# A first MLP product of 20 block products instead of 24, and a list schedule for the whole program

## The chip, the cores and the metric

The kernel runs on one core of one Trainium2 chip. The metric is device time in microseconds (us): the median over several executions. The span of a profile is a little shorter than the time of its run (608.1 for 609.9), because the time also covers start and end.

## The reference, cut to what matters

A gated linear attention (a recurrence over 768 steps, for 4 x 8 heads of 48) makes x of 3072 tokens by 384. An MLP with a hard-swish gate follows. Everything is float32.

```python
state = alpha[:, :, t, :, None] * state + einsum('bhd,bhde->...', k[:, :, t], v[:, :, t])
y[:, :, t] = np.einsum('bhd,bhde->bhe', q[:, :, t], state)
...                                     # y becomes x, 3072 x 384
h = x @ w_in                            # 384 x 2048: the first product
g = h * np.clip(h + 3.0, 0.0, 6.0) / 6.0
return g @ w_out                        # 2048 x 384: the second product
```

(The first line is shortened.) The tokens go through the kernel in 24 blocks of 128, called tokens below, two to a group, so there are 12 groups.

## The kernel before

In groups 2 to 11 the first product is plain: for each of eight pairs of 128 hidden columns, three matmuls (384 = 3 x 128) of 256 tokens into one bank, then the gate on ScalarE and the multiply on VectorE. The second product runs already as seven block products on halves.

```python
def ff1(g, i):
    h = ps_t["h", g, i] = ps.tile([C, 2, GT], FP, tag="h", bufs=2, name="h_ps")
    for f in range(2):
        for kk in range(KT):
            o = (2 * i + f) * C
            nc.tensor.matmul(h[:, f], w1[:, kk, o : o + C], xT_t[g][:, kk],
                             start=(kk == 0), stop=(kk == KT - 1))
```

A fixed loop orders the program. The loads of token n+1 are issued ahead of the scans of token n; the attention steps of the token before stand in two places of a group, and each of the eight steps of a first product is followed by one of the second product of the group before.

```python
for g in range(2, NG + 1):
    for i in range(8):
        n = G * (g + 2) + i // 4
        if i % 4 == 0 and n + 1 < NCH:
            run("la.{0} lk.{0} lq.{0} lv.{0}".format(n + 1))
        if i % 4 == 0 and n < NCH:
            run("ca.{0} r.{0} k.{0} p.{0} q.{0}".format(n))
        ...
        if g < NG:
            run("f.{0}.{1} fr.{0}.{1} fg.{0}.{1}".format(g, i))
        if i < 7:
            product(g - 1, i)
```

So the products of two groups alternate, and while VectorE and ScalarE work on one, TensorE has the other.

## Time and profile before

| | before |
|---|---|
| time, median | 609.27 us (609.22 to 609.82, 3 runs) |
| span of the profile, mean granted clock | 608.1 us, 1.000 |
| TensorE, VectorE, ScalarE, GpSimd busy | 97%, 60%, 22%, 8% |
| distance of groups | 47.7 us |

```profile
SPq L513 <- DVE o L511: 246.9, 33, 17.9
```

The clock is full in every slice. The queue stands 246.9 us before stores that wait for VectorE's results (L513 is the store). That costs nothing here: its loads come a token early. Of VectorE's waits, all those for a transfer sum to 1.5 us.

### The profile page before, as it was taken

The page shows a single profiled execution, that of the slowest core. Times are in us where ns is not written, and L with a number is a line of the kernel's source. Part 1 is how long each engine was busy: PE and PEld are TensorE (multiplying, and loading weights), DVE is VectorE, ACT ScalarE, POOL GpSimd, SP SyncE. Part 2 cuts the span into 40 slices and gives each one's busy share as a digit, 9 for nine tenths or more (in the row PEclk, how much of TensorE's full clock was granted, in tenths as well). Part 3 has the DMA queues.
Part 4 walks back from the last instruction along what each step waited for, and adds up shares of the span by engine and source line. Part 5 has one row for each costly group of instructions (what it writes and reads, how often), then busy time and mean ns, then how long its engine had stood idle before and what let it go on. Part 6 is the DMA issues. An engine that isn't in the chain of part 4 may idle for free.

```text
span 608.1 us, 10549 instructions
## 1 busy us (share of the span) xinstructions
PE 588.9 (97%) x4416; PEld 527.5 (87%) x4416; DVE 362.1 (60%) x493; ACT 135.3 (22%) x227; POOL 49.8 (8%) x78
## 2 busy tenths in 40 slices
PE   6778999999999999999999999999999999999998
PEld 4667887679999998999999998999999999999997
DVE  7698979869877577467467477357446224115141
ACT  1555445011121111111111211112111111112110
POOL 2234323201000000000000000000000000000000
PEclk9999999999999999999999999999999999999999
DMA  9999998324354243132131131130000000000000
GB/s 161 195 221 183 182 237 167 90 74 94 94 126 103 67 99 83 36 80 60 40 98 44 30 75 44 29 77 13 9 14 8 8 15 7 9 19 8 6 14 27
DMA packets 90384, 44.74 MB, mean 74 GB/s; under 512 B 54752, under 2 KB 85216, under 8 KB 90336
## 3 DMA queue, kind: packets, MB, share of 16 engines
q1 hardware_dynamic: 90336, 44.06, 33.4%
q8 instruction: 35, 0.57, 0.4%
q14 instruction: 13, 0.11, 0.1%
HBM read 39.32 MB, written 4.72 MB: 72 GB/s over the span
## 4 chain that ended last, share of the span: by engine, by line
PE 81%; DVE 0%; ACT 0%; issue 0%
PE h_ps L408 35%; PE x_ps L503 19%; PE y_ps L503 14%; PE sc_ps L314 3%; PE y_ps L378 3%; PE o_ps L430 2%; PE u_ps L356 2%; PE y_ps L388 2%; PE kb_ps L331 1%; DVE raw L196 0%; DVE q L306 0%; PE tq_ps L255 0%; ACT o L509 0%
## 5 line engine op out<-in xcount | busy, mean ns | idle before, releaser
L408 PE MATMUL h_ps<-xT,w 128*128 128x256 f32 x1152 | 265.8, 382 | 7.7 <-POOL w L201 7.7
L408 PEld LDWEIGHTS h_ps<-xT,w 128*128 128x128 f32 x1152 | 214.0, 190 | 39.5 <-POOL w L201 9.6
L418 DVE SCALAR_TENSOR_TENSOR g_sb<-r,h_ps 128x512 f32<-128x512 f32 x96 | 65.6, 684 | 149.4 <-ACT r L413 149.0
L413 ACT ACTIVATE r<-h_ps,half 128x512 f32<-128x512 f32 x96 | 66.0, 687 | 224.2 <-PE h_ps L408 219.6
L503 PE MATMUL x_ps<-rings,g_sb 128*128 128x192 f32 x352 | 60.8, 326 | 0.0
L503 PE MATMUL y_ps<-w,g_sb 128*128 128x192 f32 x352 | 60.8, 326 | 0.0
L503 PEld LDWEIGHTS x_ps<-rings,g_sb 128*128 128x128 f32 x352 | 58.4, 190 | 1.0
L503 PEld LDWEIGHTS y_ps<-w,g_sb 128*128 128x128 f32 x352 | 58.4, 190 | 1.0
L341 POOL TENSOR_TENSOR t<-t,R 128x384 f32<-128x384 f32 x20 | 18.3, 917 | 388.6 <-DVE t L368 255.4
L320 DVE TENSOR_TENSOR A<-sc_ps,mask 128x512 f32<-128x512 f32 x48 | 30.9, 685 | 15.3 <-PE sc_ps L314 15.3
L282 DVE TENSOR_TENSOR_SCAN R<-t,ones 128x516 f32<-128x516 f32 x24 | 31.2, 1304 | 11.7 <-POOL t L341 9.1
L314 PEld LDWEIGHTS sc_ps<-q,k 48*128 48x128 f32 x384 | 24.7, 197 | 7.9 <-issue 5.9
L293 DVE TENSOR_TENSOR_SCAN P<-t 128x516 f32<-128x516 f32 x24 | 31.0, 1294 | 0.5
L314 PE MATMUL sc_ps<-q,k 48*128 48x128 f32 x384 | 29.4, 295 | 1.1 <-DVE q L306 1.1
L503 PE MATMUL x_ps<-rings,s 128*128 128x192 f32 x176 | 30.4, 326 | 0.0
L503 PE MATMUL y_ps<-w,s 128*128 128x192 f32 x176 | 30.4, 326 | 0.0
L503 PE MATMUL x_ps<-w,g_sb 128*128 128x192 f32 x176 | 30.4, 326 | 0.0
L503 PEld LDWEIGHTS x_ps<-w,g_sb 128*128 128x128 f32 x176 | 29.2, 190 | 0.6
L503 PEld LDWEIGHTS y_ps<-w,s 128*128 128x128 f32 x176 | 29.2, 190 | 0.5
L503 PEld LDWEIGHTS x_ps<-rings,s 128*128 128x128 f32 x176 | 29.2, 190 | 0.5
L396 ACT COPY xT<-y_ps 128x384 f32<-128x384 f32 x24 | 11.5, 478 | 79.3 <-PE y_ps L388 66.9
L378 PE MATMUL y_ps<-A,t 128*32 128x128 f32 x768 | 27.0, 282 | 0.3 <-DVE A L320 0.3
(76 smaller groups left out, 491.1 us busy)
## 6 DMA issues: line engine op xcount, KB each, us to landing
raw<-in_moe_w_out_dram SPq DMA_DIRECT2D x8, 768.0 KB, 4.7
t<-in_v_dram SPq DMA_DIRECT2D x48, 96.0 KB, 3.4
raw<-in_moe_w_in_dram SPq DMA_DIRECT2D x24, 192.0 KB, 7.0
out_dram<-o SPq DMA_DIRECT2D x44, 96.0 KB, 1.7
aq<-in_alpha_dram SPq DMA_DIRECT2D x32, 96.0 KB, 2.4
raw<-in_k_dram SPq DMA_DIRECT2D x32, 96.0 KB, 2.3
raw<-in_q_dram SPq DMA_DIRECT2D x32, 96.0 KB, 2.3
aq<-in_alpha_dram SPq DMA_DIRECT2D x32, 80.0 KB, 2.2
```

What stands on the lines that cost most here:

```text
L282: nc.vector.tensor_tensor_scan(out=reverse(R, n - 1, n), data0=reverse(ax, n, n), data1=reverse(ones, n, n), initial=0.0, op0=ALU.mult, op ...
L293: nc.vector.tensor_tensor_scan(out=P_t[j], data0=aX[j % 2][:, 0:n], data1=ini[j % 2], initial=0.0, op0=ALU.mult, op1=ALU.add)
L314: nc.tensor.matmul(sc[h % 2][:, h // 2], K_t[j][r, h // 2], Q_t[j][r, h // 2], start=True, stop=True)
L320: nc.vector.tensor_tensor(out=A_t[j][:, NP * o : NP * (o + 1)], in0=ps_t.pop(("sc%d" % o, j)), in1=mask.unsqueeze(1).to_broadcast([C, NP, ...
L341: nc.gpsimd.tensor_tensor(out=st[j % 2], in0=sm[j % 2], in1=R_t[j][:, :, 0:1].to_broadcast([C, NP, 2 * D]), op=ALU.mult)
L356: nc.tensor.matmul(u[:, p], kb_t[j][:, p], both, start=True, stop=True)
L378: nc.tensor.matmul(y[32 * p : 32 * p + 32, (i + 1) // 2], vs[:, 2 * p + a, 32 * e : 32 * e + 32], A[:, NP * a + p], start=(i == 0), stop=( ...
L388: nc.tensor.matmul(ps_t["y", j][32 * p : 32 * p + 32, kk], st[j % 2][:, p, 32 * kk : 32 * kk + 32], Q_t[j][:, p], start=False, stop=(kk == ...
L408: nc.tensor.matmul(h[:, f], w1[:, kk, o : o + C], xT_t[g][:, kk], start=(kk == 0), stop=(kk == KT - 1))
L413: nc.scalar.activation(out=r_t[g, i], in_=ps_t["h", g, i], func=AF.Relu, bias=half, scale=1.0 / 6.0)
L418: nc.vector.scalar_tensor_tensor(out=gs[g % 2][:, 2 * i : 2 * i + 2], in0=r_t.pop((g, i)), scalar=1.0, in1=ps_t.pop(("h", g, i)), op0=ALU. ...
L503: nc.tensor.matmul(to[g], lhs[:, f], rhs[:, f], start=(first and f == 0), stop=(last and f == HF - 1), skip_group_check=True)
```

## The change

It has three parts. The product of the group's x (2 x 3 blocks of 128 x 128) by W1 (3 x 4 blocks of 128 x 512) is made from 20 products of sums of blocks, where the plain way has 24. The tables tell which sums; eleven of the twenty intermediate sums in PSUM are copied out by ScalarE, and each of the eight output blocks is then put together by adds, of which four a group go to GpSimd. The groups no longer alternate: group g's first product is followed by its second, and both share one buffer of g. And the fixed loop is replaced by a word list for the whole program that a list scheduler made offline.

```diff
-    NV = 4
+    NV = 3
-    FIRST = 8
+    FIRST = 6
+    NQ = 2
...
+    W_SUMS = [(12, 4, 1, 9, 1), (13, 4, 1, 8, -1), ...          # 25 sums of W1 blocks
+    X_SUMS = [(1, 1, 2, 1), (1, 1, 4, -1), ...                  # 11 sums of x blocks
+    PRODUCTS = [(11, 19, True, False), (12, 2, False, False), ...   # x, w, start, stop
+    OUTPUTS = [[(8, 1), (4, 1)], [(9, -1), (2, -1)], [(6, -1), (1, -1), (13, -1)], ...
...
+    def product1(g, i, m=None):
+        ...
+        for f in range(4):
+            nc.tensor.matmul(acc[g][i][:, f * C : (f + 1) * C], spots[w][:, f * C : (f + 1) * C],
+                             x_of(g, x), start=(first and f == 0), stop=last,
+                             skip_group_check=True)
+
+    def keep1(g, i, z):
+        kept_t[g, i] = slots[z]
+        nc.scalar.copy(out=slots[z], in_=acc[g][i])
+
+    def output1(g, o, step):
+        (h, sh), (a, sa), *more = OUTPUTS[o]
+        at = kept_t[g, a]
+        if more and step == 0:
+            b, sb = more[0]
+            add(nc.gpsimd, at, at, 1, kept_t[g, b], sa * sb)
+        else:
+            add(nc.vector, at, acc[g][h], sh, at, sa)
+            h_t[g, o] = at
...
-    NG = NCH // G
-    for g in range(2, NG + 1):
-        for i in range(8):
...
+            ... q.23 M.10.0.0 G.9.3 O.9.3 sc.23 n.10.0.13 lv.23 M.10.7.1 m.23 M.10.1 n.10.7.10
```

A word names a step, a group (or token), an index and sometimes a bank or slot: M is a block product of the first product, n its copy, o an output add, e the gate, h the multiply, P a block product of the second product, K, G and O its copies, results and stores, s a sum of g, xc a sum of x, y a sum of W1; la, lk, lq, lv are the loads of a token.

## The prediction

> **What bounds the kernel now.** I read the page first: the busy shares, the 40 slices and the chain that ended last.
>
> ```profile
> PE 588.9 (97%) x4416; PEld 527.5 (87%) x4416; DVE 362.1 (60%) x493; ACT 135.3 (22%) x227; POOL 49.8 (8%) x78
> ...
> PE   6778999999999999999999999999999999999998
> PEld 4667887679999998999999998999999999999997
> DVE  7698979869877577467467477357446224115141
> ...
> PE 81%; DVE 0%; ACT 0%; issue 0%
> PE h_ps L408 35%; PE x_ps L503 19%; PE y_ps L503 14%; PE sc_ps L314 3%; PE y_ps L378 3%; PE o_ps L430 2%; PE u_ps L356 2%; PE y_ps L388 2%; PE kb_ps L331 1%; DVE raw L196 0%; DVE q L306 0%; PE tq_ps L255 0%; ACT o L509 0%
> ```
>
> TensorE is the bound from the sixth slice on (about 75 us), and L408, the first MLP product, is the largest part of its chain. VectorE is at 70 to 90% in the first 120 us and near 60% after. Busy TensorE is not TensorE at its pace, so I went to the timeline for start-to-start times.
>
> ```profile
> 33.21 0.60 PE L255 MATMUL ta_ps<-ident,rings 128*128 128x128 f32 x4
> ...
> 301.06 2.76 PE L408 MATMUL h_ps<-xT,w 128*128 128x256 f32 x12
> 303.65 2.76 PE L503 MATMUL y_ps<-w,g_sb 128*128 128x192 f32 x16
> 306.25 1.03 PE L356 MATMUL u_ps<-t,kb 128*128 128x96 f32 x8
> ```
>
> The columns are start, length, engine, line, operation, shapes, count. One matmul from start to end is 0.379 us at 256 columns, 0.326 at 192, about 0.273 at 128 or 96. So the pace is (2.76-0.379)/11 = 0.216 us at 256 columns, (2.76-0.326)/15 = 0.162 at 192, (0.60-0.273)/3 = 0.109 at 128 and (1.03-0.275)/7 = 0.108 at 96; single starts of the last are 0.112 apart after the first. It falls with the columns, 0.84 ns each, down to 128; at 96 it stays[...]. The trace has 1152 matmuls at L408 where the code calls 576, so a float32 matmul is two instructions.
>
> [...] a scan of 1.23 us takes 2.27 beside a GpSimd add.
>
> ```profile
> 110.18 1.46 POOL L201 TENSOR_TENSOR w<-raw 128x768 int32<-128x768 int32 x1 [7.73 <-DVE raw L196]
> 110.47 2.27 DVE L282 TENSOR_TENSOR_SCAN R<-t,ones 128x516 f32<-128x516 f32 x1
> ```
>
> **The change, part by part.**
>
> (1) First product, groups 2 to 11. Before: 8 x 2 x 3 x 2 = 96 instructions at 0.216 us = 20.7 us a group. After: 20 products x 4 blocks x 2 = 160 at 0.110 us = 17.6. TensorE saves 3.1 us a group on the path, 31 us in ten groups. Groups 0 and 1 stay as they were.
>
> (2) Waits inside the accumulation. Eleven of the twenty products are followed by a copy of their bank. From the first matmul of a product to the first of the next in that bank: 7 x 0.110 + 0.275 (last matmul) + 0.03 (hand-over) + 0.585 (a 128x512 ScalarE copy, as at L336) + 0.05 = 1.71 us. The schedule puts another product (0.88 us) or an attention step between, so 0.88 + 0.88 = 1.76 covers it; where scores alone stand between (about 0.5 us), 0.3 is lost. I count 0.4 us a group, 3 us in eight groups.
>
> (3) The end of a group. Product 13 is followed by copy, GpSimd add (about 1.05 us, between 0.83 for 384 and 1.46 for 768 elements), VectorE add 0.69, gate 0.69, multiply 0.69, before second product 1 may start: 0.77 + 0.275 + 0.59 + 1.05 + 3 x 0.69 + hand-overs 0.2 = 5.0 us from its first matmul. In the schedule of groups 4 and 7 products 13, 14, 15 of the next group and one update step stand there, 3.7 us: 1.3 lost in each. In the other attention groups more than 5 us of work stands there. Group 10 has three products, 2.6 us: 2.4 lost. Group 11 has 13 and 14 alone and also bare waits of 0.83 us before products 11, 13 and 14: 5 us. Sum 10 us.
>
> (4) VectorE. Added per group: eight output adds from PSUM (0.69 each, 5.5 us) and eleven adds of 128 elements, about 0.29 each by the slope from 192 (0.357) to 512 elements (0.685), 3.2 us. The sums of g in halves add 0.4. That is 9.1 us on the 28.6 to 29.4 that it works per 48 us now:
>
> ```profile
> 231.00:279.00 48.00, 48.00 (x355) 43.96 (x354) 28.57 (x37) 9.22 (x17) 0.83 (x1) 1.00 0.26 63
> 279.00:327.00 48.00, 48.00 (x379) 44.24 (x378) 29.37 (x39) 9.16 (x17) 1.67 (x2) 1.00 0.26 64
> ```
>
> (Columns: stretch, length, then busy time of TensorE matmul, weight load, VectorE, ScalarE, GpSimd, each with its count.) So about 38 of a group of 45 us: 85%, no bound by itself. ScalarE gets 11 x 0.585 = 6.4 us more, 16 of 45. GpSimd gets four adds, 4.2 us, [...]perhaps 2 us of VectorE a group, mostly in its slack: 2 us in all on the path.
>
> (5) The start. 25 sums of W1 (128x512, 0.69 us, 17 us), and tokens 6 and 7 change from TensorE transposes (24 x 0.109 = 2.6 us) to six VectorE ones (1.1 us each, 6.6 us). VectorE has 24 us more where it is nearly full. Part fits: it is only 57% busy from 120 to 136 us (9.2 of 16), while TensorE does the plain second products; part of the sums falls behind the first new product. Estimate: 5 us later, less 1 us for the transposes.
>
> (6) The order. TensorE's gaps in the first 120 us, start-to-start against the paces above, sum to about 27 us, but come from weight words that pass ScalarE, VectorE and GpSimd in turn, which stays. I give the new order 3 us there. In the middle the old order loses only about 1.5 us a group, at the switches between attention and MLP; nothing to gain.
>
> Sum: 609.3 - 31.3 + 3 + 10 + 2 + 5 - 1 - 3 = 594, rounded up to **595 us** (2.3% less).
>
> **The rivals.** (a) The weight load paces 128-column matmuls. For it: u_ps at 0.112 with 96 columns, and the load rows stay near 190 ns each. Against it: transposes at 0.109. Had the load set 0.125, 160 would cost 20 us, almost all would be gone, and the time would be 618 without other luck. I give that little. (b) VectorE becomes the bound. For it: group 2 holds the rest of the W1 sums and two tokens' worth of scans, about 59 us by such a count of rows against 53 of TensorE; at 85 to 90% in later groups, in order[...], it may come late. Then a group takes 46 to 47 us, near the old 47.7, and the time is 602 to 610. Against it: neighbouring VectorE operations overlap by some 0.09 us in the trace, so rows overcount. (c) The gate chains and bank waits are hidden fully, because the list schedule was built on such durations, and the start is no later: 609.3 - 31.3 - 1 + 5 for the unavoidable end = 582. (d) Fewer products, but the end of the program has no attention left to fill with: that is in (3), and if each wait there were doubled, 8 us more.
>
> **Range and chances.** Between (c) and (b): 580 to 610, centre 595. The limit of 2% is 597, close to the centre, so the chance of faster is only a little over half: 0.57. Same 0.39. Slower needs both (a) and (b): 0.04.
>
> **What would show it.** Right: 1600 matmuls of 128x128 with starts 0.109 to 0.112 apart; matmuls of the old form (h_ps, 256 columns) down to 1152 - 10 x 96 = 192; VectorE near 480 us busy; groups 44 to 46 us apart; TensorE waits on ScalarE copies of well under 1 us each; gaps of 2 to 5 us before the second products of the last two groups. Wrong: a pace of 0.12 or more, TensorE waiting on VectorE sums or on GpSimd for over 10 us in all, or the first new product later than 145 us (the old first product of group 2 starts at 132.0).

The pace of 0.110 us in (1) stands on the 0.109 and 0.112 read from the trace. That a product waits for the copy out of its bank, in (2), was assumed; e6 below tries it. The 2 us for GpSimd in (4) are the author's estimate; the one measurement beside them is the scan of 2.27 us for 1.23.

## More of the kernel before

The prediction shows the lines of busy time and of the chain. Two more lines matter later: the granted clock in the 40 slices of the page, and the longest waits of the SP queue, which issues all loads and all output stores in one order (columns: what waited, for what, us in total, times, longest us).

```profile
PEclk9999999999999999999999999999999999999999
```

## The result, and the profile after

The kernel is correct, and it takes **619.12 us** (618.32 to 619.79, 4 runs), against 609.55 for the kernel before in the same rounds. The ratio is 1.0153, with a 95% interval of 1.0134 to 1.0172. (Ratios here compare the mean times of the fast runs of the same rounds, so they are not quite the ratio of the medians.) It counts as the same at the limit of 2%, but it is slower by 1.5%, and outside the predicted range.

The page of the kernel after, in the order in which the prediction read the other: busy time, slices, chain.

```profile
PE 579.7 (94%) x5032; PEld 536.0 (87%) x5032; DVE 471.1 (76%) x747; ACT 194.9 (32%) x335; POOL 105.2 (17%) x110
...
PE   6869999999999999989999999989999999979968
...
DVE  7798888999986985875896896886697797472361
...
PEclk9989999999999999989999999999999999989979
...
PE 61%; DVE 22%; SPq 7%; DMA 5%; issue 2%; ACT 2%; POOL 0%; DVEq 0%; POOLq 0%; ACTq 0%
```

The chain that ended last was 81% TensorE; now it is 61%, with VectorE, the SP queue and transfers in it. TensorE is not full any more, and its granted clock is below 0.9 in four of the forty slices. The last three of these are the slices in which groups 4, 10 and 11 end (group 7's end shows nothing); a slice is 15 us, so a dip to 0.8 or 0.7 can be a short stretch at half speed.

The stretch of about two groups, shown for the kernel before in the prediction (columns as there):

```profile
217.30:266.50 49.20, 47.62 (x474) 44.98 (x474) 37.76 (x62) 15.46 (x28) 7.02 (x6) 1.00 0.25 62
266.50:314.60 48.10, 45.36 (x378) 43.51 (x377) 36.68 (x57) 14.00 (x26) 7.49 (x7) 0.96 0.26 62
```

These two groups take 49.2 and 48.1 us, no less than before. VectorE works 37 to 38 us of each, as the prediction counted, and yet TensorE is no longer busy throughout.

### TensorE's time in accounts

To see where the time went, I took every TensorE matmul of a trace and measured from its start to the next start. Each shape has a pace when nothing is in its way (0.216 us at 256 columns, 0.1625 at 192, 0.112 or less at 128 or 96). What is over the pace is a *gap* where it is above 0.25 us, a *bubble* where it is less, and *half pace* where five or more matmuls in a row take about twice their pace. The sum of paces is the *work*.

| us | work | bubbles (number) | gaps (number) | half pace | span |
|---|---|---|---|---|---|
| before | 561.6 | 21.9 (241) | 16.0 (17) | 1.2 | 608.1 |
| after | 530.7 | 31.4 (358) | 39.6 (40) | 9.1 | 618.0 |
| difference | -30.9 | +9.5 | +23.6 | +7.9 | +9.9 |

The work fell exactly as meant. All of it, and 10 us more, came back as idle time and as matmuls at half speed. In the kernel before, all 17 gaps lie in the first 128 us. In the kernel after, that stage has 13.6 us of gaps, the stage from 185 to 546 us has 13.9 and the rest after 546 has 11.2.

### Three readings

**Loads that come late.** VectorE's longest waits for a transfer in the kernel after, and the longest wait of the SP queue:

```profile
DVE t L268 <- DMA aq<-in_alpha_dram: 32.2, 16, 3.8
DVE k L268 <- DMA kq<-in_k_dram: 15.8, 16, 2.5
DVE q L268 <- DMA qq<-in_q_dram: 3.0, 3, 1.0
```

```profile
SPq L642 <- DVE oh L637: 333.1, 29, 33.1
```

VectorE waits 51 us in all, once in each of sixteen tokens, at its block transpose of a token's alpha, k and q. The time line of the SP queue around one of them shows why (columns: start, length, engine, line, operation, tiles, count, and in brackets the idle time before with what ended it):

```profile
285.84 3.61 SPq L642 DMA_DIRECT2D out_dram<-oh  x3
...
290.54 1.92 SPq L246 DMA_DIRECT2D aq<-in_alpha_dram  x4
292.50 1.85 SPq L246 DMA_DIRECT2D kq<-in_k_dram  x4
294.40 1.85 SPq L246 DMA_DIRECT2D qq<-in_q_dram  x4
```

```profile
289.86 1.29 DVE L328 TENSOR_TENSOR A<-sc_ps,mask 128x512 f32<-128x512 f32 x2 [2.64 <-PE sc_ps L322]
294.52 1.12 DVE L268 STREAM_TRANSPOSE t<-aq 128x512 f32<-128x512 f32 x1 [3.37 <-DMA aq<-in_alpha_dram]
296.17 1.15 DVE L268 STREAM_TRANSPOSE k<-kq 128x512 f32<-128x512 f32 x1 [0.53 <-DMA kq<-in_k_dram]
```

The loads stand in the queue behind output stores of the group before. A store waits for VectorE's or ScalarE's result, the loads wait behind it, then twelve issues take 0.46 us each (1.85/4), 5.6 us, and VectorE stands at the transpose. It took its work in order here: in the 3.37 us that it stood at the transpose no later instruction of its list went ahead.

**The ends of groups.** Second product 1 of group 10 (the word P.10.1), and a later product of the same shape and count:

```profile
551.95 5.49 PE L621 MATMUL m_ps<-w,g_sb 128*128 128x192 f32 x16 [3.85 <-DVE g_sb L425]
...
560.10 2.76 PE L621 MATMUL m_ps<-w,g_sb 128*128 128x192 f32 x16
```

It waits 3.85 us for a multiply on VectorE, and then its sixteen matmuls take 5.49 us where others take 2.76. The chain of waits from product 14's last matmul (548.11) to 551.95:

```profile
548.20 1.29 DVE g_sb L462 x2
549.49 1.20 DVE g_sb L425 x2
550.69 0.60 DVE g_sb L568
551.29 0.61 DVE g_sb L425
```

Output 6 needs product 14, and output 2 stands behind it in VectorE's order; after these two adds come two multiplies, a sum of g and the third multiply, one after the other. From start to start, less the pace, such a gap is 2.53 us in groups 4 and 7 and 4.02 in groups 10 and 11.

**Half speed after a gap.** The sixteen slow matmuls begin half a microsecond after the gap, 0.32 us apart where the pace is 0.1625. The same happens in group 11 and, with eleven of them, in group 4; behind group 7's gap none are slow. The length alone does not sort them. Over the twelve profiles of the new order and its variants, after 140 us, of 20 gaps of 2.39 to 2.54 us (start to start, less the pace) 15 were followed by nine or more matmuls at half pace, and 5 were not; all 17 gaps of 2.7 to 4.2 us were (by eight or more); none of 31 gaps of 1.09 to 1.74 us was.

The trace's record of the granted clock shows where the gaps of 2.53 us in groups 4 and 7 differ. In the kernel after, the half-clock stretches after 40 us last 3.413 or 6.827 us (the very last is cut by the end), at a granted clock of 0.50, and they begin a whole number of 3.413 us apart (at 42.36, 271.05, 550.94 and 595.32 us: 67, 82 and 13 times 3.413). I cut the trace into stretches of 3.413 us at these points, and call that the grid below. These are pairs of its stretches at the ends of groups 4, 7 and 10 (columns: stretch, length, TensorE's busy time and count, granted clock, and two of the DMA):

```profile
267.64:271.05 3.41, 1.10 (x7) 1.00 0.00 0
271.05:274.46 3.41, 3.41 (x12) 0.50 0.00 0
407.58:410.99 3.41, 2.12 (x19) 1.00 0.00 0
410.99:414.40 3.41, 2.33 (x14) 1.00 0.00 0
547.53:550.94 3.41, 0.56 (x6) 1.00 0.00 0
550.94:554.35 3.41, 2.40 (x7) 0.50 0.00 0
```

Group 4's gap falls almost whole into one stretch, and the next has half the clock. Group 7's gap, as long, is cut in two by the grid (1.45 and 1.08 us), and the clock stays at 1.00. I counted the share of time that TensorE spends over its pace in every full-clock stretch after 140 us of the twelve profiles of the new order and its variants. All 29 stretches with more than 0.63 were followed by half clock, none of the 1554 with less than 0.60 was, and between these three of four were. This is a count made after the runs, not an experiment on the grid.

### The profile page after: what moved, and what is told of

Read it like the earlier page. It is cut to its first block, busy times and chain, and to the rows that moved or that the text cites. A ratio compares the mean times of both kernels' runs of the same rounds, so it can differ in the third digit from the quotient of the medians.

```text
span 618.0 us, 12218 instructions
## 1 busy us (share of the span) xinstructions
PE 579.7 (94%) x5032; PEld 536.0 (87%) x5032; DVE 471.1 (76%) x747; ACT 194.9 (32%) x335; POOL 105.2 (17%) x110
## 4 chain that ended last, share of the span: by engine, by line
PE 61%; DVE 22%; SPq 7%; DMA 5%; issue 2%; ACT 2%; POOL 0%; DVEq 0%; POOLq 0%; ACTq 0%
PE m_ps L621 27%; PE m_ps L521 14%; SPq L246 6%; PE m_ps L417 6%; DVE g_sb L425 4%; DMA kq<-in_k_dram 3%; PE sc_ps L322 3%; PE m_ps L443 3%; PE y_ps L386 2%; DVE q L268 2%; DVE P L302 2%; DMA qq<-in_q_dram 2%; PE u_ps L364 2%; DVE g_sb L462 2%; DVE R L291 2%
## 5 line engine op out<-in xcount | busy, mean ns | idle before, releaser
L621 PE MATMUL m_ps<-w,g_sb 128*128 128x192 f32 x704 | 129.6, 340 | 13.3 <-DVE g_sb L425 12.4
L621 PEld LDWEIGHTS m_ps<-w,g_sb 128*128 128x128 f32 x704 | 120.9, 199 | 16.1 <-DVE g_sb L425 14.5
L458 POOL TENSOR_TENSOR g_sb<-g_sb 128x512 f32<-128x512 f32 x40 | 57.4, 1436 | 241.4 <-ACT g_sb L527 224.2
L527 ACT COPY g_sb<-m_ps 128x512 f32<-128x512 f32 x110 | 64.2, 583 | 97.8 <-PE m_ps L521 90.0
L621 PE MATMUL m_ps<-rings,g_sb 128*128 128x192 f32 x528 | 92.0, 328 | 1.6 <-DVE oh L637 1.4
L621 PEld LDWEIGHTS m_ps<-rings,g_sb 128*128 128x128 f32 x528 | 87.2, 191 | 2.2 <-DVE oh L637 2.2
L521 PE MATMUL m_ps<-xc,w 128*128 128x128 f32 x640 | 83.3, 279 | 5.1 <-DVE g_sb L458 4.2
L521 PEld LDWEIGHTS m_ps<-xc,w 128*128 128x128 f32 x640 | 76.7, 192 | 7.9 <-DVE g_sb L458 5.4
L425 DVE SCALAR_TENSOR_TENSOR g_sb<-r,g_sb 128x512 f32<-128x512 f32 x80 | 57.7, 740 | 8.5 <-ACT r L421 8.3
L417 PEld LDWEIGHTS m_ps<-xT,w 128*128 128x128 f32 x192 | 37.2, 198 | 10.0 <-POOL w L207 3.8
L521 PEld LDWEIGHTS m_ps<-xT,w 128*128 128x128 f32 x320 | 38.5, 191 | 3.1 <-issue 1.8
```

The costliest lines, as they stand in the source:

```text
L425: nc.vector.scalar_tensor_tensor(out=to, in0=r, scalar=1.0, in1=h, op0=ALU.min, op1=ALU.mult)
L458: eng.tensor_tensor(out=out, in0=in0, in1=in1, op=ALU.add if s1 > 0 else ALU.subtract)
L521: nc.tensor.matmul(acc[g][i][:, f * C : (f + 1) * C], spots[w][:, f * C : (f + 1) * C], x_of(g, x), start=(first and f == 0), stop=last, s ...
L527: nc.scalar.copy(out=slots[z], in_=acc[g][i])
L621: nc.tensor.matmul(to[g], a, rhs[:, f], start=(first and f == 0), stop=(last and f == HF - 1), skip_group_check=True)
```

## The experiments

Four theories stood against each other: the late loads (A where a text uses letters), the adds on GpSimd, beside which VectorE's operations take longer (its sums of g in halves 1015 ns, against 682 in e2 without them) (B), the ends of the groups with the half speed behind them (C), and the eleven copies in each group with the bank waits that they bring (D). The edits of the order take the word list as a Python list and move words in it. Every kernel is correct unless it is said otherwise. The numbers of gaps and half pace come from the same accounts as above.

### e1_loads: the loads a token earlier

```diff
+        for j in range(8, NCH):
+            early = [f"{x}.{j}" for x in ("la", "lk", "lq", "lv")]
+            words = [x for x in words if x not in early]
+            at = words.index(f"tq.{j - 1}") + 1
+            words[at:at] = early
```

> The changed kernel with the loads of alpha, k, q and v for tokens 8 to 23 issued one token earlier (before the output stores that they stand behind in the DMA queue's order); nothing else moves. Theory A (VectorE runs late because, in order, it waits 51 us at its block transposes for loads that stand behind stores in the queue): its waits on those loads fall from 51 us to under 10, TensorE's gaps over 0.25 us in the middle (14.8 us) shrink to about 6, and the time falls from 619 to 608 to 612. Rival B (VectorE is late because it has too much work and is held by GpSimd; the waits for loads only fill time that it would spend waiting elsewhere): the load waits go, other waits grow by as much, time 616 to 619.

Measured: **609.85 us** (608.8 to 610.95), ratio 0.9968 (0.9918 to 1.0019), so 9.3 us less than the kernel after by the medians, and 11 by the ratios (1.0153 less 0.9968). (The same kernel in other rounds, e1_again below, is 8.6 us less by the medians and 9.6 by the ratios.) Gaps fall from 39.6 to 31.0 us. VectorE's waits for these loads are gone:

```profile
DVE k L268 <- DMA kq<-in_k_dram: 0.4, 1, 0.4
DVE t L268 <- DMA aq<-in_alpha_dram: 0.2, 1, 0.2
```

The kernel before issued its loads early, and the new order lost this. The late loads are shown to cost about 9 to 11 us. That the rest of the 51 us of waits fell into VectorE's slack is inferred. What is left after 185 us is nearly all at group ends: the time that TensorE waits before second products is the same as in the kernel after.

```profile
PE m_ps L621 <- DVE g_sb L425: 12.4, 4, 3.9
```

### e2_adds: GpSimd's adds on VectorE

```diff
-            add(nc.gpsimd, at, at, 1, kept_t[g, b], sa * sb)
+            add(nc.vector, at, at, 1, kept_t[g, b], sa * sb)
```

> The changed kernel with the four GpSimd adds of a group done by VectorE (40 adds of 128x512); the loads stay late. Rival B[...]: VectorE's lengthened operations (small x sums at 553 ns, g sums in halves at 1015 ns) return to 290 and 690, some 25 us of VectorE time, against 40 x 0.69 = 28 us of added work: about even; the chain before second product 1 gets 0.6 us shorter in each group, so 612 to 617. Theory A: the same load waits remain and set the pace, 616 to 620.

Measured: 621.02 us (617.79 to 623.85), ratio 1.0149 (1.0086 to 1.0212). The same as the kernel after.

### e4_both: e1 and e2 together

The diff is the sum of the two.

> Both edits. Theory A: as with the early loads alone, within 3 us of it (606 to 612). Rival B: only with both does VectorE catch up, and the pair gives clearly more than the sum of the two alone, to 600 to 606.

Measured: 611.95 us (611.54 to 612.97), ratio 1.0005 (0.9956 to 1.0054), no less than e1 alone. So moving the adds off GpSimd gains nothing, with or without the load waits. They are long (groups by line, with busy us and mean ns after the first bar; the first line is of the kernel after, the second of e2):

```profile
L458 POOL TENSOR_TENSOR g_sb<-g_sb 128x512 f32<-128x512 f32 x40 | 57.4, 1436 | 241.4 <-ACT g_sb L527 224.2
```

```profile
L458 DVE TENSOR_TENSOR g_sb<-g_sb 128x512 f32<-128x512 f32 x40 | 27.4, 684 | 3.5 <-ACT g_sb L527 3.3
```

1.44 us each, not the 1.05 that the prediction estimated, but moving them puts 27 us of work onto VectorE, and one pays for the other: VectorE's busy time is 471.1 us with the adds on GpSimd and 473.1 with them on VectorE. Without GpSimd beside it, its sums of g in halves (L585) fall from 1015 to 682 ns each and thirty of its small x sums from 553 to 286. So working beside GpSimd has a price, by estimate 25 us of VectorE's busy time (27.4 less 2.0), and what it costs in time by itself is not shown, since no run took GpSimd's adds away without giving their work to VectorE. The long gaps at the group ends stay (3.95 for 4.02 us in e4).

### e3_end: the first second product of groups 10 and 11 as filling

P.10.0 and P.11.0 are moved behind product 14, so that TensorE has 2.6 us of work while VectorE goes through its chain.

```diff
+        for g in (10, 11):
+            p = next(x for x in words if x.startswith(f"P.{g}.0."))
+            for x, after in ((p, f"M.{g}.14"), (f"K.{g}.0", f"h.{g}.2")):
+                words.remove(x)
+                words.insert(words.index(after) + 1, x)
```

> The changed kernel with second product 0 of groups 10 and 11 moved from before first product 12 to behind first product 14, where it fills the wait for the last gates. Theory C (the end of the program loses 4.0 us twice to the gate chain, and each such gap is followed by 16 matmuls at half pace, 2.6 us, since the granted clock fell): the gap goes to about 1.4 us and the slow matmuls vanish, less one more bare copy wait of 0.85 us each; together 2 x (2.6 + 2.6 - 0.85) = 8.7 us, time 610 to 612. If the slow matmuls are not caused by the gap, 3.5 us, 615 to 616.

Measured: 617.04 us (616.79 to 617.4), ratio 1.0088 (1.003 to 1.0146): 2 us gained where 8 were expected. The gap moved. With P.11.0 gone from among products 12 to 14, product 13 waits for a copy on ScalarE:

```profile
588.71 1.16 PE L521 MATMUL m_ps<-xc,raw 128*128 128x128 f32 x8 [2.23 <-ACT g_sb L527]
```

The copy of product 12 stands behind a gate in ScalarE's order, and the gate waits for VectorE. Half pace fell from 9.1 to 4.8 us, though.

### e5_ends: e1, all four group ends, copies ahead of gates

```diff
+        (the five lines of e1)
+        for g in (4, 7, 10, 11):
+            p = next(x for x in words if x.startswith(f"P.{g}.0."))
+            behind = f"M.{g}.14" if g >= 10 else f"M.{g + 1}.15.3"
+            copies = [next(x for x in words if x.startswith(f"n.{g}.{i}.")) for i in (11, 12, 13)]
+            moves = [(p, behind), (f"K.{g}.0", f"h.{g}.2")]
+            moves += [(x, f"M.{g}.{i}") for i, x in zip((11, 12, 13), copies)]
+            for x, after in moves:
+                words.remove(x)
+                words.insert(words.index(after) + 1, x)
```

> The early loads, and in groups 4, 7, 10 and 11 second product 0 moved to the end of the first products, with the ScalarE copies of products 11 to 13 put ahead of the gates in ScalarE's order (in e3 they stood behind one and made a new wait of 2.4 us). With the early loads alone these four ends lost gaps of 2.5, 2.5, 4.0 and 4.0 us and about 6 us of matmuls at half pace after them. Theory C (gap, then low clock): gaps of at most 1.5 us and no run of slow matmuls, against four more bare copy waits of 0.85; 609.9 to about 598 to 601. If the gates are late for another reason than their place (VectorE still behind), the gaps move elsewhere: 606 or more.

Measured: **605.73 us** (605.03 to 606.52), ratio 0.9912 (0.9878 to 0.9946). Better than e1 by 4 us, and 5 to 8 us over what was expected. What is left are again waits that came in place of the removed ones: 2.97 us in group 10 where a product needs a bank that an output add of VectorE has not read yet, 1.74 in groups 4 and 7 at the state update, and 2.54 in group 11.

### e6_nocopy: e1 without the 110 copies

The copy is left out, so later adds read old data. The result is wrong (relative error 10.9).

```diff
         kept_t[g, i] = slots[z]
-        nc.scalar.copy(out=slots[z], in_=acc[g][i])
```

> Wrong result on purpose: the early loads, and the 110 ScalarE copies of intermediate sums are left out (the additions read what the slots held), so no first product waits for a copy of its bank. Theory D ([...]a bubble of about 0.1 us, and eleven a group come from these copies): the small bubbles of the middle fall from 17 us to about 8, the bare waits of 0.84 us in the last group vanish, and the gate chains begin 0.6 us sooner: 594 to 598. Rival: the bubbles come from any change of product, waits or not: bubbles stay at 15 or more, 603 to 606.

Measured: 607.9 us (604.25 to 609.13), ratio 0.9927 (0.9878 to 0.9977), about 2 us less than e1. Bubbles between two products fall from 66 to 40 in the middle, but their sum only from 17.1 to 15.5 us there, and the gaps at the group ends stay (2.41, 2.41, 3.95, 4.17). The 2 us are within the noise (the intervals overlap, and the runs lie 5 us apart), and both expected ranges were missed, though the bubbles stayed as the rival had it. So the bank waits cost little, and most of the bubbles have another cause.

### e7_fill: unread matmuls before the second product 1 of groups 10 and 11

This tests the clock by itself. Twelve more 128 x 128 matmul calls (24 instructions, as each call is two in the trace: e7 has 5080 for 5032 in the kernel after), whose result nobody reads, are put in each of the two places where TensorE would idle. The chain is as long as before, and the work grows by 5.3 us.

```diff
+    def filler(g):
+        t = bank("z", g)
+        for n in range(12):
+            nc.tensor.matmul(t[:, n % NP], ident, mask, start=True, stop=True)
...
+        for g in (10, 11):
+            words.insert(words.index(f"M.{g}.14") + 1, f"z.{g}")
```

> The changed kernel with late loads, and 12 matmuls of 128x128 constants (24 instructions, 2.7 us) whose result nobody reads put before second product 1 of groups 10 and 11, inside the gaps of 4.0 us: TensorE works where it waited, nothing else changes. If the half-paced matmuls after the gaps (16 each, 2.6 us each time) come from the idle time, they go, and the time falls by about 5 us, to 614, though work was added. If they come from something else, the time is 619 or more.

Measured: 618.23 us (613.4 to 619.9), ratio 1.0103 (1.0049 to 1.0158). The spread is wide and the median is 4 us over the expected 614, so I do not lean on the time; the profile is of the fastest run (613.4). It is clear all the same: the gap is 1.34 us, and the product behind it has its full speed. The mean granted clock rose in all four runs, from 0.978 to 0.981 in the kernel after to 0.989 to 0.991.

```profile
551.15 2.87 PE L621 MATMUL m_ps<-w,g_sb 128*128 128x192 f32 x16 [1.18 <-DVE g_sb L425]
```

### e9_loads_fill and e1_again: the same test without the noise of the loads

e9 is e1 with e7's filling, e1_again is e1 unchanged, in the same five rounds.

```diff
+        (the five lines of e1, and the edit of e7)
```

> The early loads with the 12 unread matmuls of e7 in the two last gaps, 5 rounds, to be compared with e1_again of the same rounds. Gap, then low clock: no slow matmuls behind those gaps, 2 to 5 us faster than e1_again. Otherwise equal or slower.

> The early loads once more, 5 rounds, as the other half of the pair with e9_loads_fill: 609 to 611, ratio 0.997 as before.

Measured: **604.35 us** (603.62 to 606.01), ratio 0.9894 (0.9865 to 0.9922), against 610.53 us (608.92 to 613.59), ratio 0.9996 (0.996 to 1.0032), for e1_again. Twenty-four more instructions in each of two places make the program 6 us *faster*. In e1_again the product of group 10 has the same 3.85 us wait and takes 5.28 us (first line); the second is of e9:

```profile
543.79 5.28 PE L621 MATMUL m_ps<-w,g_sb 128*128 128x192 f32 x16 [3.85 <-DVE g_sb L425]
541.43 2.87 PE L621 MATMUL m_ps<-w,g_sb 128*128 128x192 f32 x16 [1.17 <-DVE g_sb L425]
```

The half speed is shown to come from the gap. From e1_again to e9, half pace falls from 8.7 to 2.9 us, while 4.6 us less gap pay for most of the 5.3 us more work.

### e8_best: copies early, output 2 ahead of output 6

From e1, with the first second product behind copy 13 in groups 4, 7 and 10, and in groups 10 and 11 output 2, which does not need product 14, ahead of output 6, which does. Only the core is shown.

```diff
+            put(f"M.{g}.14" if g == 11 else full(f"n.{g}.13."), full(f"P.{g}.0."))
+            if g < 10:
+                put(full(f"n.{g}.11."), f"kb.{j}", f"ck.{j}")
+            else:
+                put(f"o.{g}.3.0", f"o.{g}.2.0")
+                put(f"o.{g}.3.1", f"e.{g}.3", f"o.{g}.2.1", f"e.{g}.2", f"h.{g}.3", f"h.{g}.2",
+                    f"K.{g}.0", f"o.{g}.6.1", f"e.{g}.6", f"h.{g}.6")
+        put("M.10.14", "M.11.15.3", "M.11.16")
```

> Meant to beat both kernels: the early loads, and in groups 4, 7, 10 and 11 the end re-ordered by hand: copies of products 11 to 13 ahead of the gates on ScalarE, second product 0 between first products 13 and 14 (behind 14 in group 11), in groups 4 and 7 the key transposes between products 11 and 12 and their copy ahead of the gate, in group 10 the two borrowed products behind product 14, and in groups 10 and 11 output 2 ahead of output 6 on VectorE. With the early loads alone those ends lost 13.1 us of long gaps and 6 us of slow matmuls; by the durations measured 0.85 us should remain in each. 609.9 less about 15: 592 to 596, a ratio of 0.972 to 0.978 to the kernel before. If VectorE is still too late in the middle, 600 or more.

Measured: 606.48 us (603.76 to 608.62), ratio 0.9927 (0.9893 to 0.9961), 10 to 14 us over what was expected. Group 11 is as meant (1.09 and 1.46 us, no half speed). Group 10's gap went from 4.02 to 2.43 us. Yet gaps of about 2.4 us in groups 4, 7 and 10 bring half speed too:

```profile
542.77 4.47 PE L621 MATMUL m_ps<-w,g_sb 128*128 128x192 f32 x16 [2.26 <-DVE g_sb L462]
547.08 2.76 PE L621 MATMUL m_ps<-rings,g_sb 128*128 128x192 f32 x16
```

### e10_combined: what worked, joined

e1, groups 4 and 7 filled as in e5 and with the state update's copy early as in e8, group 10 filled by two products of group 11 and then P.10.0, group 11 as in e8.

```diff
+        for g, behind in ((4, "M.5.15.3"), (7, "M.8.15.3"), (10, "M.11.16"), (11, "M.11.14")):
+            put(behind, full(f"P.{g}.0."))
```

> The two orders that each left part of the gaps are joined: early loads; in groups 4 and 7 the first second-product stands behind the next group's product 15 and the copy of the token's inner matrix is not behind a gate on ScalarE; in group 10 two products of group 11 and then the first second-product stand behind product 14 (4.5 us of work against a chain of 4.2 us); group 11 as in the run before (gaps of 1.09 and 1.46 us left). Expected of the trace: no gap of over 1.5 us and no run of half-paced matmuls after 185 us outside group 11, 16 to 20 us less gap and half-paced time than the early loads alone in the gates of groups 4, 7 and 10 would give at most 8 us, so a time 8 to 11 us under the early loads alone (610 us): 599 to 602 us. If the granted clock, and not the chain, sets the end (rival: idle time anywhere is paid back as half-paced matmuls later), the time stays at 604 to 606 us although the gaps are gone.

Measured: **604.6 us** (602.88 to 605.77), ratio 0.989 (0.9858 to 0.9922); the profile's span is 603.0 us. That is 3 to 6 us over the expected 599 to 602. In groups 4 and 7 the gaps are down to 1.3 us and have no half speed behind them. Half pace is 3.7 us in all, 2.5 of it in the first stage. But in group 10 the gap moved once more, to product 14, which waits for the copy of product 13, and that stands behind a gate on ScalarE:

```profile
534.75 2.07 PE L521 MATMUL m_ps<-xc,w 128*128 128x128 f32 x8 [2.26 <-ACT g_sb L527]
```

This kernel and e9 are the fastest, both 1.1% faster than the kernel before, and some 2.6% faster than the one after (0.989 over 1.0153). Its accounts are work 530.7, bubbles 30.7, gaps 30.7 and half pace 3.7 us. Since e1 had 31.0 us of gaps, nearly all that this order gains on e1 is half pace, and the gaps only moved; 16 to 20 us less of both were expected. The time lies in the range of the rival, that idle time is paid back as half pace anywhere, but its condition, that the gaps are gone, was not met, so the run does not decide on it.

## Why the prediction was wrong

The prediction said 595 us, and its steps sum to 15.3 us less than before; the span is 9.9 us longer. No one step carries the miss of 25.2 us. Here are its terms beside what the accounts show.

| term | predicted, us | shown, us |
|---|---|---|
| (1) work of the first product, transposes, all TensorE work | -31.3 | -30.9 |
| (2) bank waits; all bubbles | +3 | +9.5 |
| (3) gaps at the ends of groups | +10 | +15.6 |
| half speed (no step) | 0 | +7.9 |
| (4) VectorE beside GpSimd; load waits | +2 | +8.0 |
| (5), (6) start | +1 | -2.4 |

(15.6 is 2.53 + 2.53 + 4.02 + 4.02 and three waits of 0.84 to 0.86 us for copies in group 11. 8.0 is the 13.9 us of gaps between 185 and 546 us, less the two of 2.53, less the 0.8 that e1 left there beside its own chain gaps. -2.4 is 13.6 less 16.0. The column sums to 7.7; 2.2 of the 9.9 us are not assigned, in part gaps of 0.9 between 128 and 185 us.)

**(1) was right.** The pace of the new matmuls is 0.112 us in the trace, predicted 0.110, and the rival (a), a pace of 0.125, falls. A saving of 31 us of TensorE's work was real, and it is in every kernel. Other signs that it named also came: 1600 and 192 matmuls, 471 us of VectorE, gaps of 4 us before second product 1 of the last two groups. The groups, at 49.2 and 48.1 us for 44 to 46, did not. (A slip in its reading: TensorE is at 9 tenths from the fifth slice on, 61 us, and not the sixth.)

**(4) is the step that failed.** It held VectorE to be "85%, no bound by itself", from the count of its work, and that count was right (37 us of a group). But a count of work says nothing about an engine whose instructions wait in order. VectorE stood 51 us at transposes whose loads were behind stores in the SP queue. e1 shows this to be worth about 9 us of time, by moving the loads alone. The rival (b) named VectorE as the possible bound but from its work and from GpSimd beside it, and e2 and e4 show no gain from taking the adds off GpSimd, though they do not price this alone. Neither step nor rival looked at where the words of the loads stand against those of the stores, although both are in the diff.

**(3) had the right mechanism and the wrong size, and lacked its second half.** It followed one output from product 13 and got 5.0 us from its first matmul. In group 10 this took 6.8 us (545.16 to 551.95), because output 6 waits for product 14 and stands ahead of output 2 in VectorE's order, and the multiplies of several outputs follow one another. So 10 us were 15.6. The second half is the clock, for which the prediction has no term at all, the largest single miss: 7.9 us more at half pace than before, of which the clock's own part is shown by e9 against e1_again. The rival (d), 8 us more by doubled waits, was in the right direction; the two together came to 13.5 us more (5.6 and 7.9).

**(2) was right in its own term, and too narrow.** e6 puts all copies together at about 2 us, within its noise, predicted 3. But bubbles of about 0.1 us at each change between attention and MLP and before products that wait for something grew from 241 to 358. The prediction read that the old order "loses only about 1.5 us a group" at such switches and found nothing to gain, and did not ask what the new order, which puts the attention pieces in one by one, would lose. From 185 to 546 us the bubbles at changes between attention and MLP grew from 35 to 69 (3.4 us more), but those between first products from 18 to 70 (4.1 us more), of which e6 took away about 30. That these changes make the bubbles is argued from where they lie in the trace; no run undid it.

**(5) and (6) erred on the other side.** The first new product starts at 128.3 us, before the old first product of group 2 (132.0), so the 25 sums of W1 and the tokens that VectorE now transposes cost nothing on the path, and the new order of the start gained a few us.

**Rival (c)**, everything hidden, was the lower end of the range, and e10 shows why it was far: with the load waits and most of the end gaps gone, 30.7 us of bubbles and 30.7 of gaps remain.

What stays open: most of the bubbles; why the times of e7 spread over 6.5 us; what GpSimd's adds cost in time by slowing VectorE; and what is left to gain with another schedule. The three parts of the change were never tried apart: no run has the twenty products in the old alternating order, or the plain products in the new order. Each of my moves of one word took a gap away and made another of 1 to 3 us elsewhere, since three engines in order wait for each other at the end of a group (in e3 TensorE waited 2.23 us for ScalarE, whose copy stood behind a gate that waits for VectorE).

## What to carry to other kernels

When a change saves work on the bound engine, look at every other engine's order, not only at its busy share: for each wait of an in-order engine or queue ask what stands ahead of it, above all loads behind stores (here 51 us of waits on VectorE, about 9 us of time). A gap on TensorE can cost more than its length: here matmuls at half pace followed all 17 gaps of 2.7 us or more, 15 of 20 near 2.4 to 2.5 us, which hung on where they fell, and none of 31 up to 1.74 us; so cut the longest gaps first, and where no work can be found, even unread matmuls in the gap can pay (6 us in e9). An order that runs a group to its end must have other work ready for exactly that place; the old one, which alternated two independent groups, had no gap over 0.25 us after 128 us. That alternating would also have saved the new products is not tested.
